# Block convolution by spectra in one Trainium2 kernel: other frequencies, tables in wide operations, products in wide operations, and a loop by frequency

## The chip, the cores and the metric

The kernel runs on one core of one Trainium2 chip. The metric is the device time of one execution in microseconds (us). Times are medians of several executions with the lowest and highest behind them. "The granted clock" (PEclk in the views) is the share of its full clock that TensorE was given in a stretch, averaged over it. One execution of each kernel was profiled; where in it a stretch starts differs by up to 2.9 us between executions of kernels that do not differ there, because the stage ahead ends at 353.6 to 356.4 us. Where a microsecond matters I therefore compare lengths of stretches and not clock times.

## The reference, cut to what matters

```python
# L = 2048 positions, D = 640 channels, N = 128 states, F = 1728, everything bf16
K  = einsum("dn,dnl,dn->dl", C, exp(dt*A*l), dt*B).real      # one kernel of 2048 taps per channel
y  = irfft(rfft(pad(u, 2L)) * rfft(pad(K, 2L)))[:L]          # causal convolution over the positions
a  = y + u * Dskip
b  = (gelu(x @ w_gate) * (x @ w_up)) @ w_down                # x is u
g  = sigmoid((x * gate_w).sum(-1))
out = g * a + (1 - g) * b
```

So there are three stages: the kernel K is generated (stage 1), u is convolved with it (stage 2, giving `a`), and a gated feed-forward network (FFN) gives `b` (stage 3). Only stage 2 is changed here.

## The kernel before

The 2048 positions are cut into NB = 4 blocks of S = 512. A spectrum of a block has T = 1024 points (512 samples, zeros behind). In real arithmetic this gives NT = 9 tiles of 128 rows: four pairs of cosine and sine tiles, and a ninth for the last frequency alone. The transforms are matmuls with tables `FW` (forward) and `FI` (inverse), and these tables are computed on the chip, tile after tile, each from several small operations on VectorE and one sine on ScalarE:

```python
for kind in range(2):                       # FW, then FI
    for a in range(4):
        # ... s_val: the sample numbers 128*a .. 128*a+127
        for mt in range(NT):                # mt == 8 is done apart (cut)
            nc.vector.tensor_scalar(out=fv[:], in0=col_f[:], scalar1=float(128 * tt), ...)
            nc.vector.tensor_tensor(out=v[:], in0=fv[:], in1=s_val[:].to_broadcast([128, 128]), op=ALU.mult)
            nc.vector.tensor_scalar(out=v[:], in0=v[:], scalar1=off, ...)
            angle_negfrac(nfq[:], v[:], [128, 128])     # three more operations: fraction of a turn, fp32
            nc.scalar.activation(out=dst, in_=nfq[:], func=ACT.Sin, scale=sin_scale)
            # ... FI: one more operation that scales by 2/T
```

Then all four kernel blocks are transformed, and after them each output block c is done from end to end:

```python
for b in range(NB):
    fwd_block(K_sb, lambda k, b=b: 4 * b + k, Kf, b)     # 9 tiles: 8 matmuls and a ScalarE copy each
for c in range(NB):
    # ... load u block c, a_sb = u * Dskip
    fwd_block(ub, lambda k: k, Uf, c)
    for i in range(c + 1):                               # pairs of blocks with i + j == c
        for t in range(4):
            # 6 or 8 operations of 128x640 on VectorE: complex product of U[i] and K[j], added to Sc
        # ... tile 8: 1 or 2 operations
    if c > 0:
        for mt in range(NT):                             # second half of the block before, first half of this
            nc.vector.scalar_tensor_tensor(out=Mc[:, mt, :], in0=Sprev[:, mt, :], scalar=sgn[:],
                                           in1=Sc[:, mt, :], op0=ALU.mult, op1=ALU.add)
    for mo in range(4):
        # 18 matmuls FI x Mc into pY (PSUM)
        nc.vector.tensor_tensor(out=a_sb[:, tcx, :], in0=a_sb[:, tcx, :], in1=pY[:], op=ALU.add)
    Sprev = Sc
```

A product of two spectra gives 1024 samples, twice a block. Its second half belongs to the next output block. A shift by 512 samples is a sign (-1)^f in a 1024-point spectrum; `Mc` does this shift and sum.

Stage 3 begins with loads into buffers that are placed where stage 2's buffers were, so they can start only when stage 2 has released them.

```python
xT = fp.tile([128, nkt, L], BF16, name="xT")
for kt in range(nkt):                                    # five transposing transfers
    nc.sync.dma_start_transpose(out=xT[:, kt, :], in_=u2[:, kt * 128:(kt + 1) * 128])
Wg = fp.tile([128, nkt, F], BF16, name="Wg")
nc.sync.dma_start(out=Wg[:], in_=B_w_gate.rearrange("(k p) f -> p k f", p=128))
# ... Wu, Wd the same way; the first matmul of the FFN (pGt) needs xT and Wg
```

## Time and profile before

| | us |
|---|---|
| median before, first 6 executions | 836.38 (835.96 to 838.39) |
| span of the profiled execution | 834.6 |
| stage 1, kernel generation | 0 to 355.8 |
| stage 2: tables and first spectra | 355.8 to 434.0 |
| stage 2: products, inverses | 434.0 to 597.8 |
| gap: loads for stage 3 | 597.8 to 618.8 |
| stage 3 | 618.8 to 834.6 |

The view of busy time by stretch of the kernel before. The columns are the stretch, its length, the busy time of each engine with the number of its instructions, the granted clock, and the load of the DMA engines.

```profile
core 0: us, PE busy (x) PEld busy (x) DVE busy (x) ACT busy (x) POOL busy (x), PEclk, DMA share, GB/s
0.00:355.80 355.80, 185.74 (x1681) 90.18 (x1700) 307.13 (x429) 288.45 (x229) 5.76 (x25) 0.82 0.07 11
355.80:434.00 78.20, 46.91 (x294) 25.03 (x301) 73.71 (x485) 41.39 (x109) 0.00 (x0) 0.81 0.08 21
434.00:597.80 163.80, 83.06 (x554) 44.78 (x563) 159.20 (x356) 24.22 (x35) 0.00 (x0) 0.76 0.03 9
597.80:618.80 21.00, 0.03 (x1) 0.06 (x2) 0.00 (x0) 0.00 (x0) 0.00 (x0) 0.60 1.00 257
618.80:748.30 129.50, 126.11 (x629) 57.38 (x640) 99.72 (x270) 89.20 (x167) 0.00 (x0) 0.99 0.09 31
```

Read the rows that start at 355.80 and 434.00 first: VectorE (DVE) is busy for 73.71 of 78.20 us and for 159.20 of 163.80 us, and TensorE (PE) for 60% and 51% of them. Stage 2 is bound by VectorE in both of its parts. The row from 597.80 is a gap in which no engine computes and the DMA engines are fully busy. The last row is bound by TensorE.

Two lines of the waits of that kernel: which instruction waited for which, us in total, times, longest.

```profile
PE pY L470 <- DVE Mc L461: 78.3, 8, 49.0
PEld L470 <- DVE Mc L461: 49.2, 1, 49.2
```

TensorE's inverse waits 78.3 us for the combination `Mc`, which VectorE makes last. This is the confirmation that VectorE is ahead of TensorE in the chain, not behind it.

The groups of VectorE's instructions within stage 2 of the kernel before (busy us, mean ns of one, idle time before):

```profile
L461 DVE SCALAR_TENSOR_TENSOR Mc<-Sc,sgn 128x640 bf16<-128x640 bf16 x27 | 21.8, 874 | 0.0
L343 DVE SCALAR_TENSOR_TENSOR nfq<-kMs,taus 128x128 f32<-128x128 f32 x64 | 16.3, 283 | 0.0
L381 DVE TENSOR_SCALAR vang<-vang 128x128 f32<-128x128 f32 x64 | 12.0, 216 | 0.0
...
L440 DVE TENSOR_TENSOR ptmp<-Uf,Kf 128x640 bf16<-128x640 bf16 x24 | 11.1, 480 | 0.0
L433 DVE TENSOR_TENSOR Sc<-Uf,Kf 128x640 bf16<-128x640 bf16 x16 | 7.7, 482 | 0.0
```

A table operation of 128 fp32 elements lasts 216 to 283 ns, a bf16 product of 640 elements, five times as many, 480 ns. `Mc` takes 874 ns for the same 640 elements.

### The profile page before, as it was taken

What the parts mean: (1) busy time and instruction counts of PE and PEld (TensorE: products, weight loads), DVE (VectorE), ACT (ScalarE), POOL (GpSimd) and SP (SyncE); (2) the same over time, 40 slices, a digit from 0 to 9 for tenths busy, and PEclk for the clock granted to TensorE, in tenths of its full rate; (3) what the DMA queues carried; (4) which work ended last, traced back from release to release, by engine and by line L of the source; (5) the groups of instructions that cost most, each with busy time, mean ns of one, the idle gap of its engine ahead of it and who ended that gap; (6) DMA issues with size and microseconds to landing.
All of it is one profiled execution on the core that took longest, in us unless ns stands there. A gap on an engine that the chain in (4) does not pass through costs nothing.

```text
span 834.6 us, 9851 instructions
## 1 busy us (share of the span) xinstructions
PE 509.9 (61%) x3597; PEld 252.2 (30%) x3652; DVE 670.9 (80%) x1580; ACT 456.6 (55%) x560; POOL 5.8 (1%) x25
## 2 busy tenths in 40 slices
PE   0056646755675565416979960500539999998886
PEld 0021313332332322303545530200214444444443
DVE  5979898899999998699979999999417778884333
ACT  1139999999999999625753420000016666661111
POOL 2000000000000000000000000000000000000000
PEclk9998779786976896667999995755859999999999
DMA  3000000000000000100011100000391000000000
GB/s 63 0 0 0 1 1 14 13 1 13 14 13 1 13 13 0 27 13 1 2 64 32 33 1 0 0 0 0 62 332 53 1 1 1 0 1 32 33 32 31
DMA packets 44656, 19.06 MB, mean 23 GB/s; under 512 B 37248, under 2 KB 43328, under 8 KB 44608
## 3 DMA queue, kind: packets, MB, share of 16 engines
q1 hardware_dynamic: 44608, 18.44, 8.7%
q8 instruction: 28, 0.46, 0.2%
q14 instruction: 20, 0.16, 0.1%
HBM read 9.91 MB, written 2.62 MB: 15 GB/s over the span
## 4 chain that ended last, share of the span: by engine, by line
DVE 40%; ACT 35%; PE 17%; issue 3%; DMA 3%; SPq 2%; ACTq 0%; DVEq 0%
PE pD L549 8%; ACT c L267 4%; ACT e L254 4%; ACT c L265 4%; ACT p L269 4%; ACT sg L539 4%; DVE sg L540 3%; DVE Mc L461 3%; DVE q L537 2%; ACT p L268 2%; ACT c L266 2%; PE pY L470 2%; DVE HT L541 2%; DMA Wu<-in_B_w_up_dram 2%; ACT L249 2%
## 5 line engine op out<-in xcount | busy, mean ns | idle before, releaser
L531 ACT CAST Gs<-pGt 128x512 bf16<-128x512 f32 (+1 forms) x56 | 32.2, 577 | 128.1 <-PE pGt L525 127.7
L257 DVE TENSOR_SCALAR kM<-pph 128x512 f32<-128x512 f32 x120 | 79.6, 683 | 22.4 <-PE pph L253 14.6
L525 PE MATMUL pGt<-xT,Wg 128*128 128x512 bf16 (+1 forms) x269 | 70.3, 387 | 24.8 <-DMA Wg<-in_B_w_gate_dram 21.8
L470 PE MATMUL pY<-Mc,FI 128*128 128x128 bf16 (+1 forms) x211 | 36.6, 324 | 78.8 <-DVE Mc L461 78.3
L258 DVE SCALAR_TENSOR_TENSOR p<-kM,pph 128x512 bf16<-128x512 f32 x120 | 77.9, 676 | 0.2
L549 PE MATMUL pD<-Wd,HT 128*128 128x128 bf16 (+3 forms) x440 | 68.0, 298 | 13.1 <-ACT b_sb L552 12.6
L253 PE MATMUL pph<-RX,b_bf 128*128 128x512 bf16 x80 | 36.3, 461 | 60.4 <-DVE p L258 60.2
L528 PE MATMUL pUt<-xT,Wu 128*128 128x512 bf16 (+1 forms) x280 | 69.2, 379 | 0.4 <-ACT Us L533 0.4
L403 PEld LDWEIGHTS <-FW 128*128 128x128 bf16 x576 | 46.5, 101 | 70.5 <-ACT FW L385 27.0
L283 PEld LDWEIGHTS <-c 128*32 128x32 bf16 x640 | 44.8, 104 | 62.5 <-DVE K L285 37.7
L283 PE MATMUL psK<-c,c 128*32 128x64 bf16 x640 | 52.2, 204 | 17.6 <-DVE c L272 12.1
L403 PE MATMUL pU<-K_sb,FW 128*128 128x128 bf16 (+1 forms) x282 | 43.7, 311 | 28.2 <-ACT FW L385 25.3
L539 ACT ACTIVATE sg<-q 128x512 bf16<-128x512 bf16 (+1 forms) x56 | 35.2, 629 | 35.6 <-DVE q L537 35.3
L470 PEld LDWEIGHTS <-FI 128*128 128x128 bf16 x288 | 23.7, 102 | 101.9 <-DVE Mc L461 49.2
L285 DVE CAST K<-psK 32x512 bf16<-32x512 f32 x80 | 51.2, 671 | 3.3 <-PE psK L284 2.9
L556 DVE TENSOR_TENSOR diff<-a_sb,b_sb 128x640 f32<-128x640 bf16 x16 | 13.2, 824 | 50.4 <-ACT b_sb L552 50.4
L284 PE MATMUL psK<-p,p 128*32 128x64 bf16 x640 | 51.5, 203 | 3.1 <-DVE p L273 3.1
L549 PEld LDWEIGHTS <-HT 128*128 128x128 bf16 x448 | 34.7, 97 | 46.6 <-issue 22.3
L405 ACT CAST Uf<-pU 128x640 bf16<-128x640 f32 x36 | 24.9, 692 | 42.9 <-PE pU L403 42.9
L254 ACT ACTIVATE e<-pa 128x512 bf16<-128x512 f32 x80 | 44.5, 595 | 6.6 <-PE pa L252 6.4
L552 ACT CAST b_sb<-pD 128x640 bf16<-128x640 f32 x16 | 11.0, 690 | 66.4 <-PE pD L549 66.4
L284 PEld LDWEIGHTS <-p 128*32 128x32 bf16 x640 | 45.1, 104 | 6.4 <-issue 6.4
(167 smaller groups left out, 1150.4 us busy)
## 6 DMA issues: line engine op xcount, KB each, us to landing
K_sb<-K SPq DMA_DIRECT2D x40, 64.0 KB, 2.3
ub<-in_A_u_dram SPq DMA_DIRECT2D x4, 640.0 KB, 4.3
out_dram<-o_sb SPq DMA_DIRECT2D x16, 160.0 KB, 1.8
Wg<-in_B_w_gate_dram SPq DMA_DIRECT2D x1, 2160.0 KB, 8.7
Wu<-in_B_w_up_dram SPq DMA_DIRECT2D x1, 2160.0 KB, 13.7
Wd<-in_B_w_down_dram SPq DMA_DIRECT2D x1, 2080.0 KB, 19.2
dsk<-in_A_Dskip_dram SPq DMA_DIRECT2D x1, 160.0 KB, 3.6
Are<-in_A_A_re_dram SPq DMA_DIRECT2D x1, 160.0 KB, 3.7
```

Of the source, the lines that this page charges most:

```text
L254: nc.scalar.activation(out=et[:, :, xs], in_=pa[:], func=ACT.Exp)
L257: nc.vector.tensor_scalar(out=kM[:], in0=tau_src, scalar1=MAGIC, scalar2=None, op0=ALU.add)
L258: nc.vector.scalar_tensor_tensor(out=pt[:, :, xs], in0=kM[:], scalar=-MAGIC, in1=tau_src, op0=ALU.add, op1=ALU.subtract)
L283: nc.tensor.matmul(psK[:, ci, :], lhsT=c1[:, dl, :], rhs=c2[:, dl, :], start=True, stop=False)
L284: nc.tensor.matmul(psK[:, ci, :], lhsT=p1[:, dl, :], rhs=p2[:, dl, :], start=False, stop=True)
L285: nc.vector.tensor_copy(out=K0[:, :, ch8 * 8:(ch8 + 1) * 8], in_=psK[:].rearrange("p c x -> p x c"))
L403: nc.tensor.matmul(pU[:, d0:d0 + dn], lhsT=FW[:, k, mt, :], rhs=src[:, kidx(k), d0:d0 + dn], start=(k == 0), stop=(k == 3))
L470: nc.tensor.matmul(pY[:, d0:d0 + dn], lhsT=FI[:, kt, mo, :], rhs=Mc[:, kt, d0:d0 + dn], start=(kt == 0), stop=(kt == NT - 1))
L525: nc.tensor.matmul(pGt[:fsz, :], lhsT=Wg[:, kt, f0:f0 + fsz], rhs=xT[:, kt, toks], start=(kt == 0), stop=(kt == nkt - 1))
L528: nc.tensor.matmul(pUt[:fsz, :], lhsT=Wu[:, kt, f0:f0 + fsz], rhs=xT[:, kt, toks], start=(kt == 0), stop=(kt == nkt - 1))
L539: nc.scalar.activation(out=sg[:fsz], in_=q[:fsz], func=ACT.Sigmoid, scale=GELU_C)
L549: nc.tensor.matmul(pD[:, d0:d0 + dn], lhsT=HT[:fsz, ft, toks], rhs=Wd[:fsz, ft, d0:d0 + dn], start=(ft == 0), stop=(ft == nft - 1))
```

## The change

Four things are altered together.

1. **Other frequencies.** The spectra are taken at the 512 odd frequencies (2f+1)/2048 instead of 0 to 512 of 1024. There is no frequency that is real by itself, so there are four pairs of tiles and no ninth. A shift by 512 samples is now a factor of -i or +i, the sign depending on whether f is even or odd; each tile holds only even or only odd f, so the sign is one for the whole tile. A multiplication by i is only an exchange of real and imaginary part. So the shift and sum can be done once on the kernel's blocks (`Kc` = a block plus or minus the other part of its neighbour), and `Mc` goes.
2. **Tables in wide operations.** 24 operations of 128x512 that write int32 angles in 1/65536 turns. The lower 16 bits wrap around by themselves, so no operation is needed to take off the whole turns. 12 sines of 128x1024 read these halves.
3. **Loop by frequency.** For each of the four frequency tiles: spectra of K and u, then the products for all output blocks in operations of up to 2560 elements (the u block is broadcast). Only the last tile is done output block by output block, each followed by its inverse.
4. **Smaller ones.** u is loaded once, into `a_sb`; the scale 2/T is applied when the result is taken out of PSUM.

The intent is less work on VectorE, fewer instructions on it, and an earlier start of the products.

```diff
-        for kind in range(2):                  # about 64 x 6 to 8 operations of 128x128
-            ... (cut)
+        for tab, s0 in ((FK, 4), (FU, 0), (FI, 8)):
+            for a in range(4):
+                ph = wk.tile([128, 2, 512], I32, name="ph")
+                for q in range(2):
+                    nc.vector.tensor_scalar(out=ph[:, q, :], in0=oddf[:], scalar1=scl[:, s0 + a:s0 + a + 1],
+                                            scalar2=(16384.0 if q == 0 else 0.0), op0=ALU.mult, op1=ALU.add)
+                nc.scalar.activation(out=tab[:, a, :, :], in_=ph[:].bitcast(I16)[:, :, 0:1024:2], func=ACT.Sin,
+                                     scale=TWO_PI * FUDGE / 65536.0)
-        for b in range(NB):
-            fwd_block(K_sb, lambda k, b=b: 4 * b + k, Kf, b)
-        for c in range(NB):
-            ... products of 640, Mc, inverse of block c (cut)
+        for ft in range(NF):                   # NF = 4
+            odd = ft % 2 == 1
+            for b in range(NB):
+                for q in range(2):
+                    group(FK, K_sb, b, ft, q, (Kc if b == 0 else R)[:, q, b, :])   # 8 matmuls of 320 columns, 1 copy
+            for b in range(NB):
+                for q in range(2):
+                    group(FU, u_sb, b, ft, q, U[:, q, b, :])
+            for q in range(2):
+                op = ...                       # add or subtract, by odd and q (cut)
+                nc.vector.tensor_tensor(out=Kc[:, q, 1, :], in0=R[:, q, 1, :], in1=Kc[:, 1 - q, 0, :], op=op)
+                nc.vector.tensor_tensor(out=Kc[:, q, 2:4, :], in0=R[:, q, 2:4, :], in1=R[:, 1 - q, 1:3, :], op=op)
+            if ft < NF - 1:
+                for i in range(NB):
+                    n = NB - i
+                    for q in range(2):
+                        u = [U[:, r, i:i + 1, :].to_broadcast([128, n, D]) for r in range(2)]
+                        mac(ft, q, i, n, u[0], Kc[:, q, 0:n, :], u[1], Kc[:, 1 - q, 0:n, :],
+                            ALU.subtract if q == 0 else ALU.add, i == 0)
+            else:
+                for c in range(NB):
+                    ... u_sb *= Dskip for block c, mac(ft, q, c, 1, ...) for i <= c (cut)
+                    inverse(c)
```

`mac` is 3 VectorE operations for the first pair and 4 for the later ones.

## The prediction

> **What bounds the kernel now.** From the timeline and busy time by stretch of the 834.6 us span: kernel generation until 355.8 us (untouched), tables and convolution 355.8 to 597.8, a weight-load gap to 618.7, then the FFN (matmul-bound, untouched). In the convolution VectorE is the bound: busy 71.3 of 75 us while tables are made (355 to 430) and 156 of 161 us afterwards (436 to 597). TensorE there waits 78 us for `Mc` (waits view), at a granted clock of 0.6 between 494 and 583. ScalarE is mostly idle.
>
> **What changes, in VectorE time.** 128x640 bf16 products start every 0.40 us; 640, 2048 and 4096 elements last 0.480, 1.22 and 2.29 us, so I estimate 0.07 + 0.33 us per 640 elements.
> - Tables: about 70 us of small 128x128 operations become 24 of 128x512, one cast and 12 tiny ones: about 10 us by estimate. ScalarE's 12 sines of 128x1024, about 0.95 us each (2048 elements take 1.90), become the slower side.
> - Products: 304 operations of 640 (122 us) plus 27 `Mc` operations at 0.80 (21 us), 143 us, become 178 operations with 312 units of 640: 116 us. Element work hardly falls; fewer overheads and the loss of the slow `Mc` form save 27 us. This needs the double rate with a broadcast outer dimension. The Trainium skill, "VectorE: DVE Perf Modes", section "The perf-mode tier table", caps bf16 tensor_tensor at 2x; the 4096-element product here (2.29 us) agrees.
> - D-skip 6.4 us and 16 evictions of `pY` at 0.73 stay.
> - TensorE: forward 576 matmuls to 512 of 320 columns (64 groups at about 1.09 us), inverse 288 to 256. It hides behind VectorE except at both ends.
>
> **Critical path of the new stretch (estimate).** First sine about 358; four K tables at 362; the other eight sines hold up ScalarE's first evictions, so the K spectra are complete near 375, the first U near 378. Then VectorE runs almost without gaps: three rounds of 26 us plus 2.3 us fix-ups, to 463; the last frequency tile with D-skip, products and evictions 44 us, to 507. By the instruction order, evictions of inverse block c stand between the products of block c+1, so TensorE's 8.6 us per inverse is mostly hidden; but it restarts at a low clock after idle gaps (the skill's "TensorE: Matmul & The Clock Gate", Part 1, says idle halves the clock; this trace shows 0.6), so I add 6 us of stalls. The last inverse is bare: 10 to 11 us. End near 524, against 597.8. The weight loads still wait for the end of the whole convolution, so the 21 us gap and the FFN only shift.
>
> **Prediction:** 836.4 - 75 = about 761 us. Range 746 to 780. Faster by over 2%: 0.94; within 2%: 0.04; slower: 0.02.
>
> **What would show each step right or wrong.**
> - Groups of instructions: 2560-element products near 1.47 us (2.8 means the double rate was lost); table operations 0.35 to 0.5 us; sines near 1 us.
> - Timeline: first big product near 378, VectorE gapless until about 463; final eviction near 524.
> - Waits: `pY` evictions wait 10 to 18 us in total for the inverse; the 78 us wait for `Mc` is gone.
> - The stretch before the first FFN matmul still 21 us; FFN unchanged within 2 us.
>
> **What would make it wrong.** Broadcast products at single rate (about +70 us); strided weight loads or int16 strided sines much slower; ScalarE's order delaying the first spectra over 10 us more; a low matmul clock stretching each inverse; conversely, better overlap at both ends (-10 us).

## The result, and the profile after

The kernel after takes 757.62 us (755.87 to 757.98, 8 executions) against 836.09 us (833.79 to 838.39, 16 executions) before. The ratio is 0.9059, with a 95% interval of 0.9046 to 0.9073. (Here and below a ratio is the mean time of one kernel's runs over that of the other's of the same rounds, so it is not quite the ratio of the medians that are quoted.) The output is correct.

The same stretches in the kernel after:

```profile
0.00:355.30 355.30, 185.78 (x1681) 90.05 (x1700) 307.25 (x430) 288.45 (x229) 6.31 (x26) 0.82 0.09 18
355.30:377.40 22.10, 14.91 (x79) 8.43 (x80) 14.14 (x42) 17.63 (x21) 0.00 (x0) 0.77 0.09 13
377.40:462.40 85.00, 63.50 (x447) 44.58 (x446) 84.98 (x102) 37.87 (x55) 0.00 (x0) 0.89 0.00 1
462.40:518.70 56.30, 40.65 (x244) 26.01 (x243) 47.94 (x105) 0.00 (x0) 0.00 (x0) 0.83 0.00 1
518.70:540.00 21.30, 0.04 (x1) 0.07 (x2) 0.06 (x1) 0.00 (x0) 0.00 (x0) 0.60 0.96 253
540.00:669.40 129.40, 125.84 (x629) 57.30 (x641) 99.78 (x270) 89.23 (x167) 0.00 (x0) 0.99 0.09 31
```

Stages 1 and 3 are unchanged to 0.5 us. The stretch ahead of the first product fell from 78.2 to 22.1 us, the products and inverses from 163.8 to 141.3 us (85.00 + 56.30). The sum of the two falls, 56.1 + 22.5 = 78.6 us, accounts for the result (the medians differ by 78.5 us). In the row from 377.40 VectorE is busy for 84.98 of 85.00 us: through the first three frequency tiles it never waits. The gap before stage 3 is still there (21.3 us).

The waits of the kernel after:

```profile
PE pY L392 <- DVE M L384: 25.4, 6, 15.0
PE pGt L485 <- DMA Wg<-in_B_w_gate_dram: 22.1, 1, 22.1
DVE a_sb L396 <- PE pY L392: 8.3, 7, 2.6
```

TensorE waits for VectorE 25.4 us instead of 78.3. VectorE in turn waits 8.3 us for the inverse when it takes results out.

The groups of VectorE's instructions in the new stage 2:

```profile
L358 DVE TENSOR_SCALAR ph<-oddf,scl 128x512 int32<-128x512 f32 x24 | 10.5, 481 | 2.1 <-ACT FK L360 0.7 <-ACT FI L360 0.7 <-ACT FU L360 0.3
L377 DVE TENSOR_TENSOR M<-U,Kc 128x2560 bf16<-128x2560 bf16 x6 | 8.9, 1484 | 0.3 <-ACT U L372 0.3
...
L380 DVE TENSOR_TENSOR t<-U,Kc 128x640 bf16<-128x640 bf16 x18 | 8.7, 483 | 0.0
```

A product of 2560 elements lasts 1484 ns. The Trainium skill, "VectorE: DVE Perf Modes", section "The perf-mode tier table", gives bf16 products the double rate (1224 ns for 2048 elements); this trace agrees, and a broadcast operand does not lose it: 2560 elements at one per cycle would last about twice as long.

For most of the stretch ahead of the first product ScalarE sets the pace. Its timeline in the kernel after (start, duration, instruction, count, idle time before it):

```profile
357.44 4.01 ACT L360 ACTIVATE FK<-ph 128x1024 bf16<-128x1024 int16 x4 [10.94 <-DMA K_sb<-K]
361.45 4.01 ACT L360 ACTIVATE FU<-ph 128x1024 bf16<-128x1024 int16 x4
365.37 0.67 ACT L372 CAST Kc<-pU 128x640 bf16<-128x640 f32 x1
365.95 2.00 ACT L360 ACTIVATE FI<-ph 128x1024 bf16<-128x1024 int16 x2
367.85 0.68 ACT L372 CAST Kc<-pU 128x640 bf16<-128x640 f32 x1
...
376.70 0.69 ACT L372 CAST U<-pU 128x640 bf16<-128x640 f32 x1 [0.40 <-PE pU L370]
```

The four sines of `FK` are ready at 361.45, but the first spectrum of the kernel is taken out of PSUM only at 365.37, because the sines of the other tables stand before it in ScalarE's order. From 372 us on it is the other way round: each copy waits about 0.4 us for TensorE's next group of matmuls.

### The profile page after: what moved, and what is told of

It is laid out like the page before. It is cut to its first block, busy times and chain, and to the rows that moved or that the text cites. A ratio compares the mean times of both kernels' runs of the same rounds, so it can differ in the third digit from the quotient of the medians.

```text
span 755.4 us, 8948 instructions
## 1 busy us (share of the span) xinstructions
PE 498.7 (66%) x3518; PEld 261.2 (35%) x3556; DVE 585.2 (77%) x988; ACT 446.5 (59%) x492; POOL 6.3 (1%) x26
## 4 chain that ended last, share of the span: by engine, by line
ACT 40%; DVE 32%; PE 20%; issue 3%; SPq 2%; DMA 2%; ACTq 0%; DVEq 0%
PE pD L509 8%; ACT c L267 5%; ACT e L254 5%; ACT c L265 5%; ACT p L269 5%; ACT sg L499 4%; DVE M L384 4%; DVE t L383 4%; DVE sg L500 3%; DVE q L497 3%; ACT p L268 2%; DVE t L380 2%; DVE M L381 2%; ACT c L266 2%; PE pY L392 2%
## 5 line engine op out<-in xcount | busy, mean ns | idle before, releaser
L485 PE MATMUL pGt<-xT,Wg 128*128 128x512 bf16 (+1 forms) x269 | 70.0, 385 | 25.2 <-DMA Wg<-in_B_w_gate_dram 22.1
L283 PE MATMUL psK<-c,c 128*32 128x64 bf16 x640 | 52.0, 204 | 17.2 <-DVE c L272 11.7
L392 PE MATMUL pY<-M,FI 128*128 128x320 bf16 x256 | 42.6, 330 | 26.4 <-DVE M L384 25.4
L370 PE MATMUL pU<-K_sb,FK 128*128 128x320 bf16 x256 | 42.5, 328 | 18.2 <-ACT Kc L372 11.8
L516 DVE TENSOR_TENSOR diff<-a_sb,b_sb 128x640 f32<-128x640 bf16 x16 | 13.2, 823 | 50.1 <-ACT b_sb L512 50.1
L485 PEld LDWEIGHTS <-Wg 128*128 128x128 bf16 (+1 forms) x280 | 27.7, 100 | 60.4 <-issue 30.5
L495 DVE TENSOR_TENSOR q<-Gs 128x512 bf16<-128x512 bf16 (+1 forms) x56 | 23.4, 419 | 26.8 <-ACT Gs L491 26.8
L252 PE MATMUL pa<-RX,a_bf 128*128 128x512 bf16 x80 | 33.1, 424 | 14.9 <-ACT e L254 12.9
```

The source lines that it names most:

```text
L283: nc.tensor.matmul(psK[:, ci, :], lhsT=c1[:, dl, :], rhs=c2[:, dl, :], start=True, stop=False)
L370: nc.tensor.matmul(pU[:, h, 0:DH], lhsT=tab[:, k, q, f0:min(512, f0 + 256):2], rhs=src[:, 4 * b + k, h * DH:(h + 1) * DH], start=(k == 0), ...
L392: nc.tensor.matmul(pY[:, h, 0:DH], lhsT=FI[:, ft, q, 128 * mo:128 * mo + 128], rhs=M[:, q, ft, c, h * DH:(h + 1) * DH], start=(q == 0 and ...
L485: nc.tensor.matmul(pGt[:fsz, :], lhsT=Wg[:, kt, f0:f0 + fsz], rhs=xT[:, kt, toks], start=(kt == 0), stop=(kt == nkt - 1))
```

## The experiments

Twelve kernels were run. They were run beside executions of the kernel before on the same chip (medians 834.66 to 834.83 us). The kernel after was timed in earlier rounds, in which the kernel before took 836.09 us, 1.3 us more; so a difference from after is better taken from the ratios than from the medians. By the ratios a_last_wide is 10.8 us slower than after, a_xt 13.5 us and a_early3 20.4 us faster.

| run | median us (lowest to highest) | ratio to before [95%] |
|---|---|---|
| after | 757.62 (755.87 to 757.98) | 0.9059 [0.9046, 0.9073] |
| b_wide | 809.73 (809.26 to 812.12) | 0.9705 [0.9682, 0.9729] |
| b_wide_jit | 790.10 (789.86 to 790.46) | 0.9465 [0.9447, 0.9483] |
| b_no_mc | 816.99 (815.55 to 817.25) | 0.9783 [0.9763, 0.9803] |
| a_split | 762.46 (761.76 to 764.53) | 0.9133 [0.9113, 0.9152] |
| a_last_wide | 767.58 (766.19 to 768.51) | 0.9188 [0.9169, 0.9208] |
| a_double_k | 754.07 (753.96 to 754.30) | 0.9033 [0.9013, 0.9053] |
| a_double_k3 | 757.46 (755.65 to 758.11) | 0.9065 [0.9046, 0.9084] |
| a_double_k12 | 756.56 (755.42 to 757.78) | 0.9058 [0.9040, 0.9077] |
| a_double_ku3 | 756.46 (755.71 to 757.29) | 0.9057 [0.9043, 0.9070] |
| a_xt | 743.31 (742.68 to 744.78) | 0.8897 [0.8882, 0.8912] |
| a_early3 | 736.59 (735.03 to 737.06) | 0.8815 [0.8802, 0.8829] |
| a_early3_dk | 735.41 (735.19 to 736.77) | 0.8808 [0.8795, 0.8821] |

The theory: the gain is VectorE time taken off its chain (small table operations, `Mc`, overheads of small products), plus an early start of the products, which the loop by frequency allows. The rival: TensorE or ScalarE takes over as the bound, and the shorter VectorE work is not what is seen.

### Wide tables alone (b_wide)

The kernel before, with the table loop alone replaced; the old frequencies, the old order and the ninth tile are kept.

```diff
+        for kind in range(2):
+            for a in range(4):
+                ... 2 operations of 128x512 to int32, 1 sine of 128x1024; FI: 1 more to scale (cut)
-                for mt in range(NT):
+                for mt in (8,):
```

> The kernel before, with only its twiddle tables made the new way: 16 VectorE operations of 128x512 to int32 and 8 sines of 128x1024 from the low halves in place of about 400 small operations; everything else as before. Theory (VectorE is the bound, but the order of the work decides how much of a saving counts): VectorE's table time falls from about 70 us to about 10 us, yet only about 30 us of it are won, because the first product must then wait for all 36 groups of the kernel's forward transform on TensorE (39 us at 1.09 us a group): first product near 402 us in place of 434, total 805 us (800 to 812). Simple rival (every VectorE microsecond taken away counts): 776 us. Second rival (the gain comes from fewer matmuls and a faster matmul clock, not from VectorE): 830 us or more.

Measured 809.73 us, a gain of 25 us (ratio 0.9705). The theory's number was 805 us (800 to 812): it promised 5 us more than came. The tables took about 70 us of VectorE before, so where is the rest? The waits of this run name it (us in total, times, longest):

```profile
DVE Sc L439 <- ACT Uf L411: 26.6, 1, 26.6
```

VectorE is ready early and then stands idle for 26.6 us until the first spectrum of u is there, since the old order transforms all four kernel blocks first. The first product starts at 408.6 us instead of 434.0 (the theory said 402). TensorE is what VectorE waits for: it is busy without a gap through that time.

```profile
380.00:410.00 30.00, 30.00 (x223) 17.02 (x222) 3.42 (x9) 18.95 (x28) 0.00 (x0) 1.00 0.00 1
```

The wide tables alone turn a VectorE bound into a bound by 36 groups of matmuls and copies.

### Wide tables, and each kernel block transformed when it is needed (b_wide_jit)

```diff
-        for b in range(NB):
-            fwd_block(K_sb, lambda k, b=b: 4 * b + k, Kf, b)
         ...
+            fwd_block(K_sb, lambda k, b=c: 4 * b + k, Kf, c)
             fwd_block(ub, lambda k: k, Uf, c)
```

> As b_wide, and the kernel's forward transform of block c is done just before the input's forward transform of block c, in place of all four blocks ahead of the first product. Theory: the first product comes near 376 us; VectorE then waits for TensorE in the first two blocks (18 groups, 19.6 us, per block), and is gapless from about 396 us; total 781 us (775 to 790), so the wait seen in b_wide is mostly won back. Rival (TensorE's amount of work sets the time): no gain over b_wide.

Measured 790.10 us, 19.6 us less than b_wide. The first product starts at 381.4 us, 5 us later than the expected 376; between 403 and 493 us VectorE is busy for 89.7 of 90 us, but ahead of 403 it still has short gaps (busy for 17.2 of 21.6 us), and the total is 9 us above the expected 781, at the edge of the range. It follows that the early start of the products, and not only the cheaper tables, is a large part of what the change gains: 25 and 20 us, 45 of 78 us together, without other frequencies and without wide products.

### No `Mc` (b_no_mc)

```diff
-            if c > 0:
+            if False:
```

The second halves of the products are dropped. Its output is wrong, which doesn't matter for the time. (The comparison with the reference accepted it all the same; it is no version to use.) It shows what the 27 operations cost.

> WRONG RESULT ON PURPOSE: the kernel before without the 27 combinations of the previous block's sum (Mc = Sc). Theory: these stand on the chain with 0.80 us each, so 18 to 22 us go: 814 to 818 us. Rival (they are hidden behind TensorE): over 830 us.

Measured 816.99 us, 17.7 us less than before (the interval of the ratio, 0.9763 to 0.9803, is far from 1, though it lies on both sides of a 2% gain). The 27 `Mc` operations were busy for 21.8 us. The difference of 4 us is found in VectorE's waits for TensorE's inverse, first in the kernel before and then in b_no_mc (us, times, longest):

```profile
DVE a_sb L473 <- PE pY L470: 4.6, 3, 2.0
```

```profile
DVE a_sb L473 <- PE pY L470: 8.5, 6, 2.9
```

Without `Mc` VectorE comes sooner to the operations that take out the inverse, and waits 3.9 us longer there. So 21.8 us of work were taken away, and 17.7 us of time.

### Products cut to 640 elements (a_split)

The kernel after, where tiles 0 to 2 make the same products one output block at a time: 72 operations of 640 elements per tile instead of 30 of up to 2560.

```diff
-                        mac(ft, q, i, n, u[0], Kc[:, q, 0:n, :], u[1], Kc[:, 1 - q, 0:n, :], ...)
+                        for j in range(n):
+                            mac(ft, q, i + j, 1, U[:, 0, i:i + 1, :], Kc[:, q, j:j + 1, :],
+                                U[:, 1, i:i + 1, :], Kc[:, 1 - q, j:j + 1, :], ...)
```

> The changed kernel with the products of frequency tiles 0 to 2 cut back to 640 elements each: the same element work, 126 more instructions. Theory (the wide form saves 0.07 us of overhead per instruction avoided): 8 to 10 us slower than the changed kernel's 757.6, so 766 to 768 us. Rival (the width of the products is worth nothing, because TensorE or ScalarE bounds these rounds): within 2 us of 757.6.

Measured 762.46 us. By the ratios (0.9133 against 0.9059) that is 6.2 us more than after, or 4 to 8 us with the intervals of both; less than the expected 8 to 10 us. The profiles show that two things are added up here. From the first product to the start of the last tile VectorE never waits in either kernel, and this stretch is 93.7 us instead of 85.0: 8.7 us for 3 x 42 = 126 additional operations, 69 ns each, which is the theory's 0.07 us. The last tile, which has the same operations in both kernels, is 1.5 us shorter (54.8 us instead of 56.3), because VectorE waits there 6.9 us for the inverse instead of 8.3. Why it waits less was not tested.

The durations of single operations would have misled here: (4 x 480 - 1484) ns is 436 ns for three saved operations, 145 ns each. The distances between starts do not: a product of 640 elements starts every 0.40 us and one of 2560 every 1.40 us, so three saved operations are worth 0.20 us, 67 ns each. The Trainium skill, "VectorE: DVE Perf Modes", section on the TRN2 errata, says a large tile pays the fixed latency once where small tiles pay it each time. For its size the section has two figures: about 150 cycles at 0.96 GHz (156 ns) measured for the duration of a single operation, and 58 cycles (60 ns) in its cycle table. The durations here agree with the first; what an operation less saved is near the second, because successive operations overlap.

### The last tile in wide operations too (a_last_wide)

```diff
-            if ft < NF - 1:
+            if True:
 ...
-                    ... Dskip, products and inverse, block by block
+            if ft == NF - 1:
+                # Dskip for all blocks, then inverse(0) to inverse(3)
```

> The changed kernel with the last frequency tile done wide like the others: all D-skips, all products, and then the four inverse blocks one after another. Theory (cutting the last tile by output block hides three of the four inverses, 8.6 us each, behind products): VectorE saves 42 instruction overheads (3 us) but 3 inverses lie bare, less the 9 us of evictions that they now hide: about 15 us slower, 768 to 776 us. Rival (TensorE's inverses hide nothing that matters): faster by 3 us.

Measured 767.58 us, 10 us more than after, just under the expected 768 to 776. The waits of the final operations for the inverse rise from 8.3 us to this:

```profile
DVE a_sb L396 <- PE pY L392: 20.8, 14, 3.2
```

These are 12.5 us more; 42 operations fewer give back about 2.9 us (estimated from the 69 ns of a_split). The block-by-block end of the loop is worth about 10 us: with it, the products of block c+1 cover the inverse of block c.

### Is TensorE near the bound? Matmuls issued twice (a_double_k, a_double_k3, a_double_k12, a_double_ku3)

The first of these was meant to show how much room TensorE has: the forward matmuls of the kernel blocks are issued twice in tiles 1 to 3, 192 more matmuls. The accumulation starts anew at the second k = 0, so the result is the same.

```diff
-                for k in range(4):
+                for k in (0, 1, 2, 3) * (2 if tab is FK and ft > 0 else 1):
```

> The changed kernel, with the matmuls of the kernel's forward transform done twice for frequency tiles 1 to 3 (each group restarted, the same result): 192 matmuls of 320 columns more, 26 us of TensorE time. Theory (TensorE hides behind VectorE in these rounds): within 3 us of 757.6. Rival (TensorE's amount of work sets the time): about 784 us.

Measured 754.07 us, *faster* than after by 3.5 us by the medians and by 2.2 us by the ratios; in the profiled executions the stretch from the start of the tables to the last final operation is 159.7 us instead of 162.7. So TensorE is not the bound in the first tiles. But the doubling uses up all the room that it had there: over the tiles in which VectorE never waits TensorE is now busy for 85.00 of 85.00 us, where it was 63.50.

```profile
376.00:461.00 85.00, 85.00 (x628) 61.23 (x627) 84.94 (x102) 37.40 (x55) 0.00 (x0) 1.00 0.00 1
```

Yet more work seems to have made the kernel faster, by little (the intervals of the two ratios still overlap). In the profiles the whole gain lies in the last tile: from its start to the last final operation 52.5 us instead of 55.5. Two explanations: TensorE's pause before the inverses became shorter, so it started them at a higher granted clock; or the order of instructions moved. Two runs with part of the doubling followed:

> As a_double_k, with the doubled matmuls only in frequency tile 3 (64 more matmuls, 8.7 us), so that TensorE stays busy until just before the last tile's products. Two theories for the 3 us that a_double_k won with more work: (clock) TensorE comes to the inverse blocks at a higher granted clock because it was not idle for 15 us: then this run wins the same 2 to 4 us, 754 to 756 us, and its clock in the last tile is above the changed kernel's 0.74; (elsewhere) the gain came from the earlier rounds or is spread between executions: then 757 to 758 us.

> As a_double_k, with the doubled matmuls only in frequency tiles 1 and 2 (128 more matmuls, 17 us), so that TensorE has its long pause before the inverse blocks back. Clock theory: no gain, 757 to 758 us, clock in the last tile near 0.74. Other theory (the gain lies in the earlier rounds): 754 to 755 us.

Neither won anything (757.46 and 756.56 us), but neither took the pause away: TensorE's pause before the inverses was 8.47 and 10.35 us, against 14.99 us in after and 2.46 us in a_double_k, and the granted clock at the start of the last tile was 0.74 in both, as in after. They decided nothing by themselves. A comparison of the instruction orders then showed that in a_double_k the operations that take out inverses stand later in VectorE's order than in after (as the 35th, 40th, 43rd, 48th operation of the last part instead of the 29th, 31st, 36th, 41st). Order and clock were changed together. The fourth run was meant to separate them: with K's and u's forward matmuls doubled in tile 3 only, TensorE is busy until the inverses (the longest pause there is 0.91 us), while the order stays nearly that of after.

> After, with the forward matmuls of the last frequency tile issued twice for the kernel blocks and for the input blocks: the pause of TensorE before the inverses shrinks, while the evictions keep nearly the places in VectorE's order that they have in after. Clock theory (the shorter pause leaves a higher granted clock, so the inverses finish sooner): pause under 5 us, granted clock of the last tile 0.85 or more, waits of the final evictions for the inverse under 6.5 us instead of 8.3, time 754 to 756. Order theory (the run with all kernel matmuls doubled won because its evictions stood later in VectorE's order): the clock may rise, the time stays at 757 to 758.5.

Measured 756.46 us, between what the two theories had said (754 to 756, 757 to 758.5); the intervals of the ratios of this run (0.9043 to 0.9070) and of after (0.9046 to 0.9073) are nearly the same. Busy time by stretch of a_double_ku3 in the last tile, and the line of its waits:

```profile
467.00:480.00 13.00, 12.26 (x90) 8.59 (x89) 13.00 (x29) 0.00 (x0) 0.00 (x0) 1.00 0.01 1
480.00:500.00 20.00, 16.05 (x97) 10.31 (x95) 18.11 (x40) 0.00 (x0) 0.00 (x0) 0.83 0.00 1
```

```profile
DVE a_sb L396 <- PE pY L392: 8.1, 6, 2.6
```

For comparison, two stretches of after, and one stretch and the waits of a_double_k:

```profile
462.40:480.00 17.60, 13.40 (x78) 8.52 (x78) 16.58 (x38) 0.00 (x0) 0.00 (x0) 0.74 0.00 1
480.00:500.00 20.00, 15.95 (x104) 10.61 (x103) 18.86 (x43) 0.00 (x0) 0.00 (x0) 0.91 0.00 1
```

```profile
478.60:498.60 20.00, 17.73 (x123) 11.84 (x122) 20.00 (x44) 0.00 (x0) 0.00 (x0) 1.00 0.00 1
```

```profile
DVE a_sb L396 <- PE pY L392: 5.7, 4, 2.6
```

At the start of the last tile the clock rose from 0.74 to 1.00, and VectorE's waits stayed at 8.1 us in all. The timelines show that they moved. In after, 6.2 of the 8.3 us are the bare inverse of the last block, 1.0 us falls into the first inverse and 1.1 us into the third. In a_double_ku3 the wait in the first inverse is gone, but those in the third are 1.8 us. The granted clock was lower there than in after: 0.83 against 0.91 from 480 to 500 us, and 0.50 against 0.71 from 490 to 495 us, where these waits lie. The Trainium skill, "TensorE: Matmul & The Clock Gate", Part 1, describes how an idle pause halves the clock. The traces agree with that (0.50 from 603 to 618 us, in the gap of the kernel before). So a high clock at the start of the last tile is worth at most about 1 us of waits here, and by itself did not shorten this run.

In a_double_k VectorE has no wait before the last block at all. It comes later to each inverse there, but the clock of the middle stretch is higher too, 1.00. The clock at the start is excluded as the only cause; the order and the clock later on were not separated, since no run changed the order alone. a_early3_dk below repeated the win only in part, so neither explanation is shown.

### The gap before stage 3 (a_xt, a_early3, a_early3_dk)

The gap of 21 us did not change, as predicted. What is it made of? The transposing transfers and the weights queue up behind the release of stage 2's buffers. In the first run `xT` is put in the place of `K_sb`, which is dead after the forward transforms:

```diff
-        xT = fp.tile([128, nkt, L], BF16, name="xT")
+        xT = K_sb[:].rearrange("p t d -> p (t d)").rearrange("p (k l) -> p k l", k=nkt)
```

> After, with the transposed input of the last stage stored in the place of the kernel tile K_sb, which is dead after the forward transforms, so the five transposing transfers (about 12 us) may run before the convolution ends. If the 22-us gap before the last stage is the queue of transfers that wait for the buffers: gap 9 to 10 us, about 12 us won, 744 to 747. If the gap is the weight transfer alone: no gain, 757.

Measured 743.31 us, 14.3 us less than after (13.5 by the ratios; the wait of the first FFN matmul fell by 13.2 us). The issues of the transposing transfers, first in after and then in a_xt (min, median, max ns, first and last start us):

```profile
L450 SPq DMA_TRANSPOSE xT<-in_A_u_dram x5: 2173/2645/2664, 518.0 to 528.4; - x5
```

```profile
L450 SPq DMA_TRANSPOSE K_sb<-in_A_u_dram x5: 1819/2097/2438, 422.3 to 444.2; - x5
...
PE pGt L485 <- DMA Wg<-in_B_w_gate_dram: 8.9, 1, 8.9
```

They now run some 75 us before the end of the convolution (by their last start, 444.2 us against the last final operation at 518.8); what is left of the gap, 8.9 us, is the transfer of `Wg` alone. The gap was a queue of transfers that could not start earlier, one kind after the other. The DMA engines were busy throughout it (share 0.96), so a shorter transfer would have helped as well; but they had next to nothing to do in the 140 us before (share 0.00), and there the same transfers cost VectorE no time, as the next run shows.

In the second run nothing that the first FFN matmuls need waits for the end of stage 2: `Wg` takes the place of the two forward tables, `Wu` has a place of its own and is loaded during the second frequency tile, and the scratch of the tables moves into `M`, which is not yet in use.

```diff
-        Wg = fp.tile([128, nkt, F], BF16, name="Wg")
+        Wg = FUK[:].rearrange("p (k f) -> p k f", k=nkt)      # FUK holds FU and FK before
-        Wu = fp.tile(...); nc.sync.dma_start(out=Wu[:], ...)  # in stage 3
+        Wu = persist.tile([128, 5, F], BF16, name="Wu")
+            if ft == 1:
+                nc.sync.dma_start(out=Wu[:], in_=B_w_up.rearrange("(k p) f -> p k f", p=128))
+        # odd_i, oddf and ph lie inside M, declared ahead of the tables
```

> After, with the transposed input in the place of K_sb, the gate weights in the place of the two forward tables, and the up weights loaded during the second frequency tile: nothing that the first matmuls of the last stage need waits for the end of the convolution. Gap under 2 us, 20 to 21 us won, 736 to 739; rival (the transfers slow the convolution, or the last stage starts at a low clock and gives part back): 742 to 750.

Measured 736.59 us, 21.0 us less than after (20.4 by the ratios). Busy time by stretch of this run:

```profile
377.30:463.00 85.70, 62.94 (x447) 44.35 (x446) 85.68 (x104) 37.87 (x55) 0.00 (x0) 0.88 0.25 57
...
518.00:540.00 22.00, 20.76 (x153) 9.82 (x152) 11.35 (x31) 12.62 (x23) 0.00 (x0) 0.84 0.34 102
```

The first FFN matmul starts at 517.9 us, 0.9 us after the last final operation of the convolution has started. The loads now run in the first stretch (DMA share 0.25 where it was 0.00), and VectorE is not disturbed: still busy without a gap. About 2 us are given back: the stretch from the first FFN matmul to the second part of stage 3 is 131.4 us (517.9 to 649.3) instead of 129.4, at a granted clock of 0.84 at its start where it was 0.92.

The last run adds the doubled matmuls of a_double_k to this kernel.

> The previous run with the kernel blocks' forward matmuls of tiles 1 to 3 issued twice as in the run that won 3 us by doing so; VectorE's order is that run's. If that win was real and adds up: 3 us under the previous run, 733 to 736. If it was chance or is taken back by transfers: within 1 us of the previous run.

Measured 735.41 us, 1.2 us less, with overlapping intervals. That is between the two expectations; the waits for the inverse were 6.8 us, all in the last block, against 7.4 us in a_early3. Whether the order is worth 1 us, 3 us or nothing stays open. As a version to keep, a_early3 is the better one: 0.8815 of the time of the kernel before, 98 us less, without matmuls that compute nothing new.

## Why the prediction was right

It said 761 us with a range of 746 to 780, and 757.62 us were measured.

- **"VectorE is the bound."** Right. After the change it is busy for 84.98 of 85.00 us through three of four tiles, and 192 more forward matmuls (a_double_k) cost nothing, though they filled TensorE's time there.
- **Tables: 70 us become 10 us.** The 24 operations took 481 ns each (10.5 us in all), within the predicted 0.35 to 0.5 us, the sines 1.00 us each. But b_wide shows that this alone is worth 25 us, not 60: the rest is won only when the spectra come in another order.
- **First big product near 378.** It started at 377.4. The prediction had seen in the instruction order that ScalarE's sines would hold up the first copies, and the timeline shows just that.
- **Products: 143 us to 116 us.** The gapless stretch was predicted to end at 463 and ended at 462.4. `Mc` was counted at 21 us and was worth 17.7 us by itself, because VectorE then waits 3.9 us longer for the inverse. The estimate of 0.07 us per operation held where VectorE never waits: a_split paid 8.7 us for 126 operations, 69 ns each. Over the whole kernel it paid less, since the last tile gave 1.5 us back.
- **Last tile and last inverse: the term that was mis-sized.** The prediction put 44 us of VectorE's work, "6 us of stalls" for the low clock after pauses and 10 to 11 us for the bare last inverse one after the other, with an end near 524. In the trace the first is 44.7 us and the last 9.5 us; the stalls ahead of the last inverse are 2.2 us. That is most of the difference: the last final operation ended at about 518.8, 5 us early, and the time was 3.4 us under the predicted 761. The waits in all were 8.3 us, expected 10 to 18. The clock was low as feared (0.74 at the start of the last tile), but VectorE was busy with products for most of that stretch: it waited 1.0 us in it, and this wait went away where the clock was 1.00 (a_double_ku3).
- **"The 21 us gap and the FFN only shift."** Right: 21.3 us and 129.4 us, against 21.0 and 129.5 before. a_xt and a_early3 show that the gap could go.

Not all of the 78 us are accounted for one by one. The single terms that runs isolated are 25 us (tables), 20 us (order of the spectra), 17.7 us (`Mc`, by a run that is wrong) and 6 us (width), together 69 us; the remainder of about 10 us, in which the ninth tile that fell away, the operations for `Kc` that were added and the smaller changes (point 4 above) lie, was not run by itself, and these terms need not add up exactly.

## What to carry to other kernels

Before counting what a cheaper stage saves, ask what the freed engine meets next: here the cheap tables gave 25 us alone and 45 us once the first products no longer waited for spectra that were needed much later. When small operations are merged, count the saving by the distance between starts of successive operations (0.067 us each here, and 0.069 us measured where the engine never waits), not by the difference of their durations (0.145 us); and look whether a later wait takes part of it back. And look at every stretch in which no engine computes: a gap of 21 us before the next stage fell to nothing by placing its first buffers where data of the stage before had already died.

## What the Trainium skill lacked or had wrong

- "VectorE: DVE Perf Modes", section "The perf-mode tier table": there is no row for a scalar_tensor_tensor. With bf16 tensors and an fp32 scalar per partition (`sgn`) it took 874 ns for 640 elements where a tensor_tensor took 480 ns. Whether the operation or its fp32 scalar costs the double rate was not tested.
- "TensorE: Matmul & The Clock Gate", Terms: the penalty of a throttled clock is given as the throttled time times the missing share. For the first 17.6 us of the last tile in after (clock 0.74) that is an estimated 4.6 us (17.6 x 0.26). In a_double_ku3, where the clock there was 1.00, one wait of 1.0 us was gone, and the time did not change measurably. What the kernel lost here was only what something else waited for.
- No page that I found has a duration for a sine that reads every second 16-bit integer: 128x1024 took 1.00 us in the timeline (four in 4.01 us).
